# RetNet attention into a gated MLP on one core: two product groups moved ahead of the sixth piece's transposition

## The chip, the cores and the metric

The kernel runs on one core of one Trainium2 chip, in one launch. The metric is device microseconds of one execution; less is better. Each time quoted as a median comes from several executions of the same program.

## The reference

Batch 8, 8 heads, 576 positions, head dimension 64. Each head has a decay of its own, and there is no softmax. The attention's result is laid out as 4608 tokens by 512 features and goes through an MLP with 2048 hidden features. The weights arrive in double precision.

```
gamma = 1 - 2 ** (-5 - arange(H))
scores = q @ k.T / sqrt(D)
Dmat = where(i >= j, gamma ** (i - j), 0)
x = ((scores * Dmat) @ v)          # B,H,S,D -> (B*S, H*D)
h = x @ w_in
g = h * erf(softplus(h))
out = g @ w_out
```

## The kernel before

**Pieces.** The 4608 tokens are cut into 36 pieces of 128 tokens. Two batches make nine pieces: four of 128 positions for each batch, and one that holds the last 64 positions of both. Below, T5 is the transposition of the piece with index 5, which is the sixth piece; S5 are its scores and O5 its outputs.

**Stages of the attention.** Three functions handle a piece. `transposes(i)` turns q and k with four TensorE transposes each (line 332), which ScalarE copies out of PSUM (lines 334 and 338). It also has GpSimd weigh the piece's v (line 313), and at its end it issues the load of q for piece i+2. `scores(i)` multiplies the turned k and q on TensorE (line 347), and VectorE masks them into `sT`. `outputs(i)` multiplies `sT` with v (line 365), adds the product of q and the state carried from earlier pieces (line 376), and computes the new state's sum (line 388). VectorE then scales the results into the tile `x`, and the load of k and v for piece i+3 is issued. The list `stages` holds these calls in the order T0, S0, T1, O0, S1, T2, O1, S2 and so on; `attend` runs the next one. For piece 5 and piece 7 two neighbours are swapped, so that the list runs T5, O4, S5, O5, T6, S6.

**Blocks of the MLP.** Four pieces fill one tile `x` of 512 tokens, called a chunk here. There are nine chunks and four groups of 256 + 256 hidden features, so 36 blocks. Most blocks compute x @ w_in by seven products of half size (line 496). The first block of all, `firsts[0]`, uses `plain()` (line 550) instead: four accumulators in PSUM, `p0`, `p1`, `pe` and `pg`, each for one half of the tokens and one half of the group's features. The sum over 512 input features is cut into four quarters, `dc` = 0 to 3. In each quarter four groups of matmuls follow one another, one for each accumulator, and `plain()` yields after each group. A group is four matmuls of 128x256; the trace has two records for each matmul. Groups `p0` and `p1` read the tokens of pieces 0 and 1, groups `pe` and `pg` the tokens of pieces 2 and 3.

**Weights.** `load_weights` issues the transfer of one part of the weights into the tile `wraw`. `rounding()` turns a part from double to single precision in steps: ScalarE (lines 254 and 255), then VectorE (lines 259, 263, 267, 272), then a product and a sum (lines 274 and 275), on VectorE for the first group's w_in and on GpSimd otherwise. Each quarter of the first block needs one part, in `wa`.

**Order of the work.** Engines run their instructions in program order, and the program order around the change is written by hand, as one letter per call:

```
for what in "alkakakawkakakawwaa3awa2aaa5ppappa5wwppa5ppawappwcppa5ppaaapp5s":
    if what == "a":
        attend(done[0] + 1)
    elif what == "p":
        next(products)
```

Here `a` is the next stage of the attention, `p` the next group of the first block, `w` the issue of a weight part, a digit so many steps of rounding, `k` two small matmuls that only keep TensorE working, `l` a load of k and v, `c` a load of constants, and `s` the store of the first chunk. All loads named here are issued on SyncE, in program order.

Of the kernel before, what the change touches and what calls it, by code (L numbers as in the profile page):

```python
# [54 lines left out]
def kernel(  # L55
# [94 lines left out]
    def load(i, names="qkv"):  # L150
        if i < len(pieces):
            t = loaded.setdefault(i, {})
            for name in names:
                src = {"q": q, "k": k, "v": v}[name]
                if name == "q" and i < SQUARES:
                    t["q"] = load_rows(i, "q", q, 2)
                elif name == "q":
                    t["qs"] = load_squares(i, "q", q)
                    if i >= SQUARES_K:
                        t["ks"] = load_squares(i, "k", k)  # L160
                elif name == "v" or i < SQUARES_K or len(pieces[i]) == 1:
                    t[name] = load_rows(i, name, src, 4)
# [69 lines left out]
    def load_weights():  # L232
        part = next(coming, None)
        if part is not None:
            t = wraw.tile([P, 2 * WP], UINT32, tag="wraw", name="wraw")
            for rows, src in part[0]:
                nc.sync.dma_start(out=t[rows].rearrange("p (h f) -> p h f", h=2), in_=src)
            words.append((t, *part[1:]))
# [49 lines left out]
    def round_weights(n=1):  # L288
        for _ in range(n):
            next(round_step, None)  # L290
# [159 lines left out]
    def attend(upto):  # L450
        while done[0] < min(upto, len(stages)):
            of, i = stages[done[0]]
            of(i)
            done[0] += 1
# [9 lines left out]
    def store_x(c):  # L464
        nc.sync.dma_start(out=xd[c], in_=x[0, c][:, :n_dc])
# [269 lines left out]
    def keep_busy(n):  # L735
        for _ in range(n):
            nc.tensor.matmul(idle[:, :P], lhsT=ones, rhs=ones, start=True, stop=True)
# [13 lines left out]

    for what in "alkakakawkakakawwaa3awa2aaa5ppappa5wwppa5ppawappwcppa5ppaaapp5s":
        if what == "a":
            attend(done[0] + 1)
        elif what == "p":
            next(products)
        elif what == "s":
            store_x(0)  # L760
        elif what == "l":
            load(2, "kv")
        elif what == "c":
            nc.sync.dma_start(out=cst[:, CONST_FIRST:], in_=consts[:, CONST_FIRST:])
        elif what == "w":
            load_weights()
        elif what == "k":
            keep_busy(2)
        else:
            round_weights(int(what))  # L770
# [93 lines left out]
```

## Time and profile before

| what | value |
|---|---|
| median of 6 runs | 1029.72 us |
| the six runs, in order of size | 1028.46, 1029.05, 1029.40, 1030.04, 1030.07, 1030.37 us |
| profiled execution, its time | 1030.37 us |
| profiled execution, its span | 1028.6 us |
| TensorE busy | 1019.3 us, 99% of the span |
| VectorE busy | 669.0 us, 65% |
| ScalarE busy | 390.3 us, 38% |
| GpSimd busy | 122.5 us, 12% |
| mean granted TensorE clock | 0.998 |

The span is the time from the first to the last recorded instruction of the profiled execution; its own time is 1.77 us longer, for what lies around the span. All positions given below count from the span's start. PE stands for TensorE, PEld for its weight loads, DVE for VectorE, ACT for ScalarE, POOL for GpSimd, SP for SyncE. A busy PE is not PE at full rate: matmuls are pipelined, and the ends in the trace are modelled. A line of the timeline gives start, duration, engine, line of the code, operation, what is written from what, shapes and the count of records; the bracket at its end gives idle time of the engine before it and what ended it.

### The profile page before, as it was taken

The numbers are of one execution on the slowest core, as the hardware profiler recorded it, in microseconds if no ns is written. First come the engines' busy times: TensorE is split into PE (matmuls) and PEld (weight loads), VectorE is DVE, ScalarE is ACT, GpSimd is POOL, SyncE is SP. The second block draws the span as 40 slices with busy tenths as digits, with TensorE's granted clock in tenths as the row PEclk, the third lists the DMA queues.
The fourth block names the chain that finished last, engine by engine and source line by source line (L and its number), as shares of the span: only waits on it lengthen the run. The fifth ranks groups of instructions, "written<-read, shape, count | busy, mean of one in ns | idle before, by whom it ended". The sixth has DMA issues, their size and how long they took to land.

```text
span 1028.6 us, 15959 instructions
## 1 busy us (share of the span) xinstructions
PE 1019.3 (99%) x6348; PEld 876.4 (85%) x6348; DVE 669.0 (65%) x1062; ACT 390.3 (38%) x481; POOL 122.5 (12%) x122
## 2 busy tenths in 40 slices
PE   9999999999999999999999999999999999999998
PEld 7788888888888888888888888888888888888887
DVE  3759877877876666666566666666667655555555
ACT  2354133232244544343443344444443333333332
POOL 2133121222311110000001001100100000000000
PEclk9999999999999999999999999999999999999999
DMA  9996979989984444444445344444433334444434
GB/s 198 205 241 143 245 172 230 232 173 249 239 178 153 159 144 143 144 166 161 163 143 174 136 143 147 159 166 144 143 123 123 123 125 131 131 132 131 128 85 120
DMA packets 146986, 165.76 MB, mean 161 GB/s; under 512 B 97376, under 2 KB 121568, under 8 KB 138848
## 3 DMA queue, kind: packets, MB, share of 16 engines
q1 hardware_dynamic: 144832, 163.57, 56.2%
q10 hardware_dynamic: 2080, 1.18, 0.5%
q8 instruction: 50, 0.82, 0.4%
q14 instruction: 24, 0.20, 0.1%
HBM read 117.52 MB, written 47.19 MB: 160 GB/s over the span
## 4 chain that ended last, share of the span: by engine, by line
PE 90%; DMA 4%; DVE 3%; SPq 2%; issue 1%; POOL 1%; ACT 0%; DVEq 0%; POOLq 0%
PE a L604 23%; PE a L496 22%; PE g L604 12%; PE g L496 11%; PE e L496 6%; PE e L604 6%; PE s L347 3%; PE o L365 3%; PE o L388 1%; PE o L376 1%; DMA raw_v<-in_v_dram 1%; DMA raw_ks<-in_k_dram 1%; SPq L147 1%; PE f L668 1%; DMA raw_k<-in_k_dram 1%
## 5 line engine op out<-in xcount | busy, mean ns | idle before, releaser
L496 PE MATMUL a<-x,wa 128*128 128x256 f32 x1088 | 258.3, 380 | 0.0
L496 PEld LDWEIGHTS a<-x,wa 128*128 128x128 f32 x1088 | 205.8, 190 | 28.5
L604 PE MATMUL a<-wb,s 128*128 128x256 f32 x840 | 200.0, 381 | 0.0
L604 PEld LDWEIGHTS a<-wb,s 128*128 128x128 f32 x840 | 158.4, 190 | 22.9 <-ACT o L618 0.7
L99 DVE TENSOR_TENSOR t<-g,t 128x512 f32<-128x512 f32 x68 | 46.9, 690 | 150.7 <-ACT t L526 113.1
L496 PE MATMUL g<-x,wa 128*128 128x256 f32 x544 | 129.2, 380 | 0.0
L496 PEld LDWEIGHTS g<-x,wa 128*128 128x128 f32 x544 | 102.8, 190 | 14.4
L99 DVE TENSOR_TENSOR o<-a,o 128x512 f32<-128x512 f32 x104 | 71.4, 686 | 46.5 <-PE a L604 46.5
L521 ACT COPY t<-a 128x512 f32<-128x512 f32 x34 | 19.9, 586 | 188.2 <-PE a L496 188.2
L99 DVE TENSOR_TENSOR t<-t,s 128x1024 f32<-128x1024 f32 x72 | 88.8, 1273 | 0.0
L565 ACT ACTIVATE s<-t 128x1024 f32<-128x1024 f32 x72 | 72.1, 1048 | 28.4 <-DVE t L99 28.4
L274 POOL TENSOR_TENSOR wraw<-wraw 128x512 f32<-128x512 f32 x28 | 29.4, 1051 | 439.5 <-DVE wraw L272 177.9
L99 DVE TENSOR_TENSOR x<-x 128x512 f32<-128x512 f32 x115 | 75.8, 692 | 1.2
L532 ACT COPY t<-a 128x512 f32<-128x512 f32 x34 | 19.9, 586 | 144.3 <-PE a L496 144.3
L569 ACT ACTIVATE s<-s 128x1024 f32<-128x1024 f32 x72 | 72.2, 1049 | 0.4
L604 PE MATMUL g<-wb,s 128*128 128x256 f32 x280 | 66.7, 381 | 0.2 <-DVE t L99 0.2
L604 PE MATMUL e<-wb,t 128*128 128x256 f32 x280 | 66.6, 381 | 0.0
L604 PE MATMUL a<-wb,t 128*128 128x256 f32 x280 | 66.6, 381 | 0.0
L604 PE MATMUL g<-wb,t 128*128 128x256 f32 x280 | 66.4, 380 | 0.0
L496 PE MATMUL e<-x,wa 128*128 128x256 f32 x272 | 64.8, 381 | 0.0
L99 DVE TENSOR_TENSOR sT<-s,cst 128x512 f32<-128x512 f32 x72 | 46.1, 681 | 27.8 <-PE s L347 27.8
L99 DVE TENSOR_TENSOR o<-g,o 128x512 f32<-128x512 f32 x70 | 47.9, 684 | 21.5 <-ACT o L618 18.8
(86 smaller groups left out, 1249.5 us busy)
## 6 DMA issues: line engine op xcount, KB each, us to landing
od<-o SPq DMA_DIRECT2D x54, 512.0 KB, 3.3
x<-xd SPq DMA_DIRECT2D x27, 1024.0 KB, 4.8
o<-od SPq DMA_DIRECT2D x27, 1024.0 KB, 5.0
raw_qs<-in_q_dram SPq DMA_DIRECT2D x96, 112.0 KB, 4.4
raw_ks<-in_k_dram SPq DMA_DIRECT2D x84, 112.0 KB, 4.2
xd<-x SPq DMA_DIRECT2D x9, 1024.0 KB, 5.3
raw_v<-in_v_dram SPq DMA_DIRECT2D x64, 128.0 KB, 4.5
wraw<-in_moe_w_in_dram SPq DMA_DIRECT2D x32, 256.0 KB, 5.8
```

The costliest lines, as they stand in the source:

```text
L99: nc.vector.tensor_tensor(out=out, in0=in0, in1=in1, op=op)
L147: queue.dma_start(out=t[r0 : r0 + n, e::2, :], in_=heads.rearrange("h p d -> p h d"))
L274: engine.tensor_tensor(out=r_f, in0=high_f, in1=r_f, op=ALU.mult)
L347: nc.tensor.matmul(ps[e][:, p, :], lhsT=t["kT"][heads[e], p, :], rhs=t["qT"][heads[e], p, :], start=True, stop=True)
L365: nc.tensor.matmul(o[p % 2][heads[(e + p) % 2], p // 2, :], lhsT=t["v"][:, 2 * p + e, :], rhs=t["sT"][:, e, p, :], start=(p < 2), stop=(no ...
L376: nc.tensor.matmul(o[p % 2][heads[(e + p) % 2], p // 2, r0 : r0 + m], lhsT=state[heads[e], p, :], rhs=t["qT"][heads[e], p, r0 : r0 + m], s ...
L496: nc.tensor.matmul(acc[:, j * TH : (j + 1) * TH], lhsT=weights["wa", self.g][:, a, d, j * P : (j + 1) * P], rhs=x[self.g, self.c][a][:, d, :],
L521: nc.scalar.copy(out=self.t1[:, 1], in_=self.a)
L532: nc.scalar.copy(out=self.t2[:, 0], in_=self.a)
L565: nc.scalar.activation(self.s[:, j], t, AF.Softplus)
L569: nc.scalar.activation(self.s[:, j], self.s[:, j], AF.Erf)
L604: nc.tensor.matmul(acc[:, tp, :], lhsT=left[:, j * TH + tp * P : j * TH + (tp + 1) * P], rhs=weights["wb", self.g][:, b, j, :], start=(sta ...
```

## The change

One string changes. After the fourth piece's outputs and the scores of the fifth piece, the kernel before calls two groups of the first block's first quarter (`p0`, `p1`), then T5, then the other two groups (`pe`, `pg`), then O4. The kernel after calls all four groups first, then T5, then O4.

```
-    for what in "alkakakawkakakawwaa3awa2aaa5ppappa5wwppa5ppawappwcppa5ppaaapp5s":
+    for what in "alkakakawkakakawwaa3awa2aaa5ppppaa5wwppa5ppawappwcppa5ppaaapp5s":
         if what == "a":
             attend(done[0] + 1)
         elif what == "p":
```

On TensorE eight matmuls (two groups) and eight transposes exchange places. Nothing is added or removed. The instructions of VectorE, ScalarE, GpSimd and SyncE keep their order.

More of the change, by code (lines that the diff above doesn't have):

```diff
@@ L750 @@
     products = firsts[0].plain()
-    for what in "alkakakawkakakawwaa3awa2aaa5ppappa5wwppa5ppawappwcppa5ppaaapp5s":
+    for what in "alkakakawkakakawwaa3awa2aaa5ppppaa5wwppa5ppawappwcppa5ppaaapp5s":
         if what == "a":
```

## The prediction

> **What bounds the kernel now.** I read the page first. TensorE is busy for 1019.3 of 1028.6 us, and the chain that ended last lies on it for nine tenths:
>
> ```profile
> PE 1019.3 (99%) x6348; PEld 876.4 (85%) x6348; DVE 669.0 (65%) x1062; ACT 390.3 (38%) x481; POOL 122.5 (12%) x122
> PE 90%; DMA 4%; DVE 3%; SPq 2%; issue 1%; POOL 1%; ACT 0%; DVEq 0%; POOLq 0%
> ```
>
> So an edit pays only where TensorE stands still or runs slowly, and what it saves there is kept only if nothing later holds TensorE back. The waits of TensorE over the whole span are few. The longest is 1.6 us, for the load of q at line 332, and that is T5. The next view is TensorE's timeline around it:
>
> ```profile
> 28.62 1.16 PE L347 MATMUL s<-qT,kT 64*128 64x128 f32 x16
> 29.71 1.99 PE L550 MATMUL p<-x,wa 128*128 128x256 f32 x8
> 33.27 0.63 PE L332 MATMUL pt_q<-ident,raw_q 128*128 128x128 f32 x4 [1.57 <-DMA raw_q<-in_q_dram]
> 34.45 0.75 PE L332 MATMUL pt_k<-ident,raw_k 128*128 128x128 f32 x4 [0.56 <-DMA raw_k<-in_k_dram]
> 35.00 1.92 PE L550 MATMUL pe<-x,wa 128*128 128x256 f32 x4
> 36.71 1.78 PE L550 MATMUL pg<-x,wa 128*128 128x256 f32 x4
> 38.42 1.09 PE L365 MATMUL o<-sT,raw_v 128*64 128x128 f32 x16
> ...
> 48.70 1.89 PE L550 MATMUL p<-x,wa 128*128 128x256 f32 x8
> 50.43 1.03 PE L550 MATMUL pe<-x,wa 128*128 128x256 f32 x4
> 51.30 1.03 PE L550 MATMUL pg<-x,wa 128*128 128x256 f32 x4
> 52.25 1.16 PE L347 MATMUL s<-qT,kT 64*128 64x128 f32 x16
> ```
>
> Two things are to be seen. TensorE idles 1.57 + 0.56 = 2.13 us for the sixth piece's q and k. And `pe` and `pg` behind T5 take 38.42 - 35.00 = 3.42 us, where the same two groups of a later quarter, at 50.43, take 52.25 - 50.43 = 1.82 us, and a full set of four groups 52.25 - 48.70 = 3.55 us. The third view explains this: stretches of 3.41 us laid where the granted clock changes (columns: length, PE busy, granted clock, DMA share, GB/s).
>
> ```profile
> 7.52:10.93 3.41, 2.71 (x26) 1.00 1.34 218
> 28.00:31.41 3.41, 3.41 (x44) 1.00 1.23 212
> 31.41:34.82 3.41, 1.29 (x10) 1.00 0.80 161
> 34.82:38.24 3.42, 3.42 (x11) 0.50 0.90 182
> 38.24:41.65 3.41, 3.41 (x41) 1.00 1.11 209
> ```
>
> TensorE was busy for only 1.29 us of 31.41 to 34.82, and then the clock was halved from 34.82 to 38.24: just where `pe` and `pg` ran. A stretch that was busy for 2.71 us, at 7.52, was followed by full clock.
>
> **The change, part by part.** *The two groups go into the wait.* `p0` starts at 29.71 as now. Four groups at full clock take 3.55 us, so T5's first transpose is due at 29.71 + 3.55 = 33.26. Its q let the present one start at 33.27. The first wait is filled to the last hundredth, and T5 is not delayed at all. The wait for k stays: the k transposes start at 34.45, as now. *O4 follows directly.* From the first k transpose to the next instruction it takes 0.43 us at 48.27 and 0.53 us at 55.61; I take 0.50. O4 then starts at 34.95 instead of 38.42, which is 3.47 us earlier. At full clock the two groups would have taken about 3.55 - 1.82 = 1.73 to 1.82 us behind T5; so some 1.75 us of the gain is the filled wait and 1.7 us the half clock that does not come.
>
> *Does the clock stay up?* In 31.41 to 34.82 TensorE would now be busy from 31.41 to 33.26 (1.85 us), for the q transposes (0.63) and for the part of the k transposes before 34.82 (0.37): 2.85 us, above the 2.71 that kept full clock. I therefore count no slow stretch. A bound: if it came all the same, O4 and what follows would lose half of 3.41, 1.7 us.
>
> [...]
>
> *The wait that moves.* `pe` and `pg` read the third and fourth piece's tokens, so `pe` now waits itself for VectorE's scaling of O3. That ended at 30.23 + 0.41 = 30.64, and `pe` is due at 29.71 + 1.73 = 31.44: 0.8 us in hand. Were this cover gone, each microsecond would cost one until the k transposes' 34.45 absorb it.
>
> *Queues that T5 is moved past.* T5 also issues GpSimd's weighing of v (no place changed: it waited until 36.32 for its load) and SyncE's load of q for piece 7, which needs T5's q transposes done. SyncE gets to that load only at 39.17, 5.3 us after those transposes; they end at the same 33.9 in both kernels. So no later load is put off. ScalarE's copy of k stays at about 35.3, tied to the load.
>
> *What is late next.* O4's inputs are ready: its `sT` was written by 31.83 and its v weighed by 29.1. Behind it comes this run on VectorE and ScalarE:
>
> ```profile
> 35.30 0.58 ACT L338 COPY kT<-pt_k 128x512 f32<-128x512 f32 x1 [0.72 <-PE pt_k L332]
> 35.78 0.66 ACT L254 ACTIVATE wa<-wraw 128x512 f32<-128x512 f32 x1
> 39.57 0.42 DVE L99 TENSOR_TENSOR x<-o,cst 128x256 f32<-128x256 f32 x1 [4.23 <-PE o L365]
> 40.70 0.41 DVE L259 TENSOR_SCALAR wa<-wa 128x512 f32<-128x512 f32 x1
> 44.21 1.28 DVE L99 TENSOR_TENSOR sT<-s,cst 128x512 f32<-128x512 f32 x2
> ```
>
> VectorE stood idle for 4.23 us before 39.57, waiting for O4, so it can start 3.47 us earlier. It then rounds the third weight part, from 40.70 - 3.47 = 37.2; ScalarE has that ready by 35.78 + 0.66 = 36.44, with 0.8 us in hand. The second part, needed by `p0` of the next quarter at 39.91 - 3.47 = 36.44, is finished at 34.65 + 0.69 = 35.34. `sT` of piece 5 and O5, which waits about half a microsecond for it now, move together. Then come the loads for T6, now at 47.78 and then at 44.3: SyncE issued its k by 35.96, and transfers there take 5.7 us, so they are in by 41.7. The fourth weight part reached ScalarE at 39.21, and VectorE wants it at 45.41 - 3.47 = 41.9. The first part of w_out is issued by 43.7 and takes 5.4, in by 49; ScalarE's use moves from 49.48 to 49.0 at best, but VectorE wants it only at 54.65 - 3.47 = 51.2. From 60 to 91 VectorE is tight (the chain runs over it), but it starts those stretches behind TensorE and ScalarE, which move too. From 91 on TensorE has almost no wait left. I count nothing given back; the bound is all of it, which is the third case below.
>
> **The sum.** 1030.37 - 3.47 = 1026.90 us for an execution like the profiled one, its span 1025.1. That execution is 0.65 us above the median of 1029.72, and the six runs spread over 1.91 us. If the half clock struck in only some of them, the others gain about 1.75: the upper three (mean 1030.16) would come to 1026.7, the lower three (mean 1028.97) to 1027.2. Both meet at 1026.9, which I forecast; its own range is 1026.0 to 1027.8.
>
> **The rivals.** *Only the wait pays.* The half clock is rare without the profiler, or comes back after T5, or a part of it is absorbed. Then 1.75 us off the median gives 1028.0, off the profiled run 1028.6. For it: one execution shows the clock. Against it: the spread of 1.9 us is about what such a stretch costs.
>
> *The load was never the end of it.* VectorE's backlog from 73 to 93, or a load tied to the clock on the wall, takes the place of the wait, and the time stays near 1029.7. For it: the chain of waits passes over VectorE's rounding there. Against it: the margins above, and 3.45 us idle on VectorE at 53.45.
>
> *The rounding holds its place (slower).* If the third part's rounding stayed at 40.70 to 44.29 in spite of O4's earlier end, `sT` of piece 5 would stay at about 45.5, and TensorE, there at 41.5, would stand 3.4 us longer than now. That gives back 3.4, and a stretch with so little work would halve the clock for another 3.41 us, for 1.7 more: 1030.37 - 3.47 + 3.4 + 1.7 = 1032.0. It loses against the profiled run from an added wait of 3.47 - 1.7 = 1.8 us on. Against it: VectorE's 4.23 us idle and ScalarE's early rows.
>
> **How the numbers follow.** About 0.2%, 2.06 us, is what a measurement of this kernel can tell from no change; that is 1027.66 on the fast side. The full gain has 0.68, only the wait 0.18, nothing kept 0.10, slower 0.04. Faster by over 0.2% takes the first and a tenth of the second: 0.70. Within it: 0.26. Slower: 0.04. The range takes in the first two cases and part of the third, with half a microsecond of spread below: 1025.6 to 1029.2.
>
> **What would show it.** In the changed kernel's timeline the four groups run from 29.7 to 33.3, the wait for q is gone or under 0.2 us, the one for k stays near 0.5, and O4 starts near 35.0. The granted clock stays at 1.00 through 38. O5 waits about half a microsecond for `sT` as now, and the second product block and all later ones come 3.5 us earlier. The forecast is wrong if a wait at O5, T6 or the masks between 73 and 93 grows by over a microsecond, or if 0.50 stands anywhere in the granted clock before the end.

## The result and the profile after

The kernel after takes 1027.37 us in the median of 17 runs (1026.1 to 1031.25), the kernel before, over all runs up to then, 1030.0 us in the median of 38 (1027.89 to 1032.61). The ratio is 0.9976, with a 95% interval of 0.9969 to 0.9984; that is 2.5 us less, from 1.6 to 3.2. The forecast was 1026.9 us, with a range of 1025.6 to 1029.2.

The profiled execution of the kernel after took 1027.61 us, its span 1025.8 us. These are the lines of TensorE's timeline that answer to those shown of before (a group is two matmuls with two records each, so x4 is one group, and it is four matmuls that change places with the eight transposes):

```profile
29.72 1.99 PE L550 MATMUL p<-x,wa 128*128 128x256 f32 x8
31.55 1.03 PE L550 MATMUL pe<-x,wa 128*128 128x256 f32 x4
32.41 1.03 PE L550 MATMUL pg<-x,wa 128*128 128x256 f32 x4
34.37 0.63 PE L332 MATMUL pt_q<-ident,raw_q 128*128 128x128 f32 x4 [0.93 <-DMA raw_q<-in_q_dram]
35.40 0.63 PE L332 MATMUL pt_k<-ident,raw_k 128*128 128x128 f32 x4 [0.40 <-DMA raw_k<-in_k_dram]
35.95 1.09 PE L365 MATMUL o<-sT,raw_v 128*64 128x128 f32 x16
...
42.79 0.40 PE L365 MATMUL o<-sT,raw_v 128*64 128x128 f32 x2 [0.34 <-issue]
...
50.05 1.16 PE L347 MATMUL s<-qT,kT 64*128 64x128 f32 x16
```

`pe` and `pg` now run at full rate (1.03 us each by their records, against 1.92 and 1.78 before) in the time in which TensorE stood still. The wait for q has shrunk from 1.57 to 0.93 us and is not gone, because in this execution q landed about a microsecond later than in the profiled one of before (34.37 against 33.27). O4 starts 2.47 us earlier (35.95 against 38.42), the scores at line 347 near 50 are 2.20 us earlier (50.05 against 52.25), and the span is 2.8 us shorter. Most of the rest of that last figure comes in small steps much later: in the profile of before TensorE waits for VectorE by 0.28 us at the scores at 236.54 and by 0.20 us at the products at 255.40; after, both waits are gone, and one of 0.23 us stands at the scores at 272.62.

The third view, stretches of 3.41 us (length, PE busy, granted clock, DMA share, GB/s), laid in phase with the one change of the granted clock at the start of this trace:

```profile
31.67:35.08 3.41, 2.40 (x13) 1.00 0.83 155
35.08:38.50 3.42, 3.10 (x41) 1.00 0.85 179
```

The least busy of them has 2.40 us of work, and the clock stays at 1.00 up to the drain at the end of the kernel (0.50 from 1024.95). The prediction had 2.85 us for its stretch. Most of the difference is the later load: the k transposes start at 35.40, behind the end of the stretch, where 0.37 us of them were counted in.

### The profile page after: what moved, and what is told of

It reads as the page before. It is cut to its first block, busy times and chain, and to the rows that moved or that the text cites. A ratio compares the mean times of both kernels' runs of the same rounds, so it can differ in the third digit from the quotient of the medians.

```text
span 1025.8 us, 15958 instructions
## 1 busy us (share of the span) xinstructions
PE 1017.3 (99%) x6348; PEld 875.5 (85%) x6348; DVE 668.7 (65%) x1062; ACT 390.2 (38%) x481; POOL 122.6 (12%) x122
## 4 chain that ended last, share of the span: by engine, by line
PE 88%; DMA 6%; DVE 2%; SPq 2%; ACT 1%; issue 1%; POOL 1%; DVEq 0%; POOLq 0%; ACTq 0%
PE a L604 23%; PE a L496 22%; PE g L496 11%; PE g L604 11%; PE e L604 6%; PE e L496 5%; PE s L347 2%; PE o L365 2%; DMA raw_v<-in_v_dram 2%; DMA raw_qs<-in_q_dram 1%; PE o L388 1%; PE o L376 1%; SPq L147 1%; DMA raw_ks<-in_k_dram 1%; PE f L668 1%
```

## The experiments

There were two explanations to tell apart. Theory A: the gain has two parts, the wait that is filled and the stretch at half clock that no longer follows it. Rival B: only the filled wait pays, and the half clock in one profiled execution was an accident. Every timed execution comes with its mean granted TensorE clock; one stretch of 3.41 us at half clock lowers it to 0.998, which makes the two countable. (A mean of 0.999 need not have such a stretch: in experiments 6 and 7 it is a half clock in the last 1.1 and 1.5 us, behind the last matmul.)

**1. The kernel before, unchanged**

> The kernel before, unchanged, for the granted clock of each of its executions. Theory A (an idle wait of about 2.1 us ahead of the sixth piece's transposition, and behind it a half clock of 3.41 us that costs 1.7 us more, in a good part of the executions): at least a third of the executions show a mean granted clock of 0.998 (one half-clock stretch, 3.41 x 0.5 / 1028 = 0.0017), and these are 1 to 2 us longer than those at 0.999 to 1.0. Rival B (only the wait paid, the half clock in the profiled execution was an accident): hardly any execution is at 0.998, or those that are take no longer. Time against the kernel before: 0 +- 0.7 us.

Time: ratio 0.9994 (0.9985 to 1.0003). Together with the runs of before beside it there are 34 executions: 20 at 0.998 or lower, with a mean of 1030.57 us, and 14 above, with a mean of 1028.92. Over all three sets of runs in this study there are 71 executions of the kernel before: 38 at 0.998 or lower (mean 1030.59) and 33 above (1028.92). So the half clock strikes in 54% of the executions, and these are 1.67 us longer in the mean. Its profile caught it again, with the stretches in another phase:

```profile
32.17:35.59 3.42, 1.57 (x11) 1.00 0.65 145
35.59:39.00 3.41, 3.41 (x15) 0.50 0.87 163
```

TensorE was busy for 1.57 us of the first stretch and ran at half clock in the second. Rival B falls on this: the half clock is common and has its price.

**2. Idle work in the wait**

```
-    "...aaa5ppappa5ww..."
+    "...aaa5ppfappa5ww..."
+        elif what == "f":
+            spare = ps_at.tile([P, NP, P], FP32, tag="at", name="spare")
+            for _ in range(6):
+                nc.tensor.matmul(spare[:, 0, :], lhsT=ones, rhs=ones, start=True, stop=True)
```

> The kernel before, with six small 128x128 matmuls on constants put into the wait, ahead of the sixth piece's transposition; the order is otherwise that of before. They take about 1.3 us where TensorE stood still for 1.57 us, so they do no useful work and delay nothing. Theory A: the stretch from 31.4 to 34.8 is now busy for about 2.6 us, the clock stays at 1.00, and the kernel is 0.8 to 1.7 us faster than before (all of it from the clock). Rival B: no gain, 0 +- 0.4 us.

Ratio 0.9986 (0.9976 to 0.9995), 1.4 us less than before; none of 11 executions at 0.998. The timeline of its profile:

```profile
31.29 1.50 PE L772 MATMUL spare<-ones 128*128 128x128 f32 x12
33.22 0.63 PE L332 MATMUL pt_q<-ident,raw_q 128*128 128x128 f32 x4 [0.43 <-DMA raw_q<-in_q_dram]
34.70 1.03 PE L550 MATMUL pe<-x,wa 128*128 128x256 f32 x4
```

T5 starts when its load is in, as before; the matmuls ahead of it produce nothing that is used. Yet `pe` takes 1.03 us for its four records and not 1.92, and the kernel is faster. This is the clock's part alone. The mean of the 11 executions, 1028.68 us, is that of the kernel before without the half clock (1028.92) within the spread of the runs.

**3. Three groups ahead of T5**

```
-    "...aaa5ppappa5ww..."
+    "...aaa5pppapa5ww..."
```

> Three of the four groups ahead of the sixth piece's transposition, the fourth behind it. Theory A: each group moved into the wait saves its 0.87 us as long as the load is not yet in, and one group is enough to keep the clock up (the stretch is then busy for about 2.0 us): 1.7 to 2.6 us faster than before, the part left over being the fourth group's 0.87 us. Rival B: 0.87 us faster. If 2.0 us of work are too few to keep the clock, also about 0.9.

Ratio 0.9972 (0.996 to 0.9984), median 1027.57 us, none of 6 executions at 0.998. One group was enough to keep the clock, with 2.31 us of work in the stretch over the wait. T5 still waited 0.69 us for q and 0.41 us for k, and O4 started at 35.75. It came out no slower than the kernel after, although the fourth group fits into that wait. The profiles show how this can be: O4 starts at 35.00 in experiment 5, 0.75 us earlier than here, and yet the span is 1025.8 us there and 1025.5 us here. "What was late next", below, has the place where it was lost.

**4. O4 ahead of T5 as well**

```
-        if i in (PC + 1, 2 * PC - 1):
+        if i in (PC, PC + 1, 2 * PC - 1):        # with the string of after
```

> The kernel after, with the outputs of the fifth piece (O4, 1.5 us on TensorE) also ahead of the sixth piece's transposition. In the profile of after, that transposition still waited 0.93 us for q and 0.40 us for k. If these waits are the rest of the loss, O4 fills them and the kernel is 0.9 to 1.5 us faster than the kernel after, 3.4 to 4.1 us faster than before. If VectorE's work behind O4 decides (scaling, rounding of the third weight part, mask of piece 5), O5 waits longer for its mask and less than 0.5 us is gained over after. If the later load of piece 7's q, which now comes behind its k and v, is missed at T7, a wait at T7 appears.

Ratio 0.9967 (0.9955 to 0.998), median 1026.8 us. T5 no longer waits, but O5 does:

```profile
36.79 0.45 DVE L259 TENSOR_SCALAR wa<-wa 128x512 f32<-128x512 f32 x1 [0.95 <-ACT wa L254]
...
41.12 1.64 PE L365 MATMUL o<-sT,raw_v 128*64 128x128 f32 x16 [0.92 <-issue]
```

The mask of piece 5 stands behind the rounding of the third weight part on VectorE, and that waits for ScalarE, whose step stands behind T5's copies: VectorE idled for 0.95 us ahead of line 259. This is the mechanism of the second expectation. The gain over the kernel after is 0.6 us by the medians and 0.9 us by the two ratios, so its size does not decide between the two expectations. The third one's wait at T7 did not occur. One of 6 executions was at 0.998.

**5. The kernel after, unchanged**

> The kernel after, unchanged, for the granted clock of its executions and as the neighbour of the three that follow. Theory A (the filled wait, 1.6 us, and the half clock that does not come, 1.65 us in those executions that have it): at most one execution in eight at a mean clock of 0.998; those of the kernel before, beside it, at 0.998 in about half, and 1.65 us longer there than the others. Time: 2.2 to 2.9 us faster than before. Rival B (only the wait): as many half-clock executions as before, 1.6 us faster.

Ratio 0.9976 (0.9967 to 0.9986), median 1027.44 us, none of 9 executions at 0.998; beside it the kernel before had 8 of 19 there, with a mean of 1030.66 against 1029.17 us for the other 11. With the result's own executions (18 are listed with their clock) the kernel after has 1 of 27 at 0.998. This profile has T5 as the prediction had it:

```profile
33.43 0.63 PE L332 MATMUL pt_q<-ident,raw_q 128*128 128x128 f32 x4 [0.17 <-DMA raw_q<-in_q_dram]
34.44 0.63 PE L332 MATMUL pt_k<-ident,raw_k 128*128 128x128 f32 x4 [0.38 <-DMA raw_k<-in_k_dram]
35.00 1.09 PE L365 MATMUL o<-sT,raw_v 128*64 128x128 f32 x16
```

**6. ScalarE's step earlier**

```
-    "...aaa5ppppaa5ww..."
+    "...aaa5ppppa1a4ww..."        # with the swap of experiment 4
```

> The fourth experiment's order (four groups and O4 ahead of the sixth piece's transposition) with ScalarE's first step on the third weight part taken ahead of that piece's copies. There VectorE stood idle for 0.95 us before line 259, waiting for ScalarE, and O5 waited 0.92 us for the mask behind it. If ScalarE's place in this queue is what now ends last, VectorE starts line 259 at once, O5's wait falls to 0.2 us or less, and the kernel is 0.7 to 0.9 us faster than that one, 4.0 to 4.5 us faster than before. If the wait at O5 is VectorE's own length of work, it stays over 0.6 us and nothing is gained.

Ratio 0.9962 (0.995 to 0.9975), median 1025.64 us, 1.8 us below the kernel after on the same chip (1.4 us by the ratios). VectorE did start line 259 at once, at 36.04. But O5 still waited 0.72 us, where 0.2 or less was expected. These are the two lines of VectorE and GpSimd that show why:

```profile
36.95 1.41 DVE L267 SCALAR_TENSOR_TENSOR wa<-wraw,wa 128x512 uint32<-128x512 uint32 x1
36.50 1.32 POOL L313 TENSOR_TENSOR raw_v<-raw_v,cst 128x512 f32<-128x512 f32 x1 [6.51 <-DMA raw_v<-in_v_dram]
```

The step of line 267 takes 0.69 us elsewhere; here it began while GpSimd weighed v and took 1.41. The wait at O5 is of just that size, so it is the wait of the second expectation that stayed. Whether this kernel is faster than that of experiment 4 is not settled by the two intervals.

**7. O4 in the wait in place of the product groups**

```
-    "...aaa5ppppaa5ww..."
+    "...aaa5ppaapp5ww..."        # with the swap of experiment 4
```

> The two product groups stay behind the sixth piece's transposition as in the kernel before; the fifth piece's outputs (O4, 1.5 us) go into the wait in their place. Theory A: what fills the wait does not matter, only that it is work whose inputs are there. O4 takes 1.5 of the 1.57 us, the clock stays at 1.00, and the kernel is 2.1 to 2.8 us faster than before, as far as after. Against it, if the product groups had to go first for the sake of what follows on VectorE or ScalarE: under 1.2 us faster.

Ratio 0.9966 (0.9953 to 0.9979), median 1026.04 us, none of 5 executions at 0.998. As far as 5 executions can tell, what fills the wait does not matter. The profile shows a late load (T5 waited 1.32 us for q in spite of O4), and so it has the least busy stretch around T5 that kept the clock. The end of the same execution has one that did not; there are no transposes in it:

```profile
31.70:35.11 3.41, 1.76 (x33) 1.00 0.64 126
35.11:38.52 3.41, 3.34 (x18) 1.00 0.85 177
...
1021.57:1024.98 3.41, 1.32 (x7) 1.00 0.81 226
1024.98:1026.45 1.47, 0.00 (x0) 0.50 0.04 12
```

**8. The load earlier, the order on TensorE as before**

```
-    "...kakakawwaa3awa2aaa5ppappa5ww..."
+    "...kakakawaa3awwa2aaa5ppappa5ww..."
```

> The order of the kernel before on TensorE; on SyncE one weight part (512 KB) is loaded behind the sixth piece's q, k and v instead of ahead of them. SyncE issues that q some 1.5 us earlier, so it lands about 1.5 us earlier, and T5 waits 0 to 0.5 us instead of 1.57. Theory A: 1.2 to 1.7 us from the wait and about 1 us from the clock, 2.0 to 2.8 us faster than before with no instruction of TensorE moved. If the transfers are bound by bandwidth in a way that the order does not change, or if the third weight part now comes too late for VectorE, the wait shows up again at T5 or O5 and less than 1 us is gained.

The profiled execution is 3.07 us below that of before (1027.30 us), but the median of 11 runs is 1028.79 and the ratio 0.9994 (0.9983 to 1.0004): no gain that can be told. In the profile T5 starts at 31.27 without a wait for q, and the third weight part is late instead, so the wait has gone to O5:

```profile
42.50 1.64 PE L365 MATMUL o<-sT,raw_v 128*64 128x128 f32 x16 [1.37 <-issue]
```

3 of the 11 executions are at 0.998, with a mean of 1030.83; the other 8 have 1028.21. So the wait that was moved, not removed, seems to bring the half clock along.

**9. The kernel of experiment 6 again**

> The sixth experiment's kernel (four groups and O4 ahead of the sixth piece's transposition, ScalarE's step on the third weight part earlier) again, as neighbour of the next. 3.2 to 4.2 us faster than before, at most one execution in eight at a clock of 0.998.

Ratio 0.9968 (0.9958 to 0.9979), median 1026.15 us, none of 8 executions at 0.998. The ratios of both sets, 0.9962 and 0.9968, lie below the kernel after's 0.9976 by 0.8 to 1.4 us.

**10. The mask ahead of the rounding**

```
-    "...aaa5ppppa1a4wwppa5ppawapp..."
+    "...aaa5ppppa1awwppa4ppa5wapp..."        # with the swap of experiment 4
```

> That kernel with piece 5's mask ahead of the rounding of the third weight part on VectorE, and the rounding of the fourth part behind piece 5's outputs. O5 waited there for the mask, by 0.72 us and half a microsecond more inside its first matmuls, because the rounding stood in front and one step of it took 1.41 us instead of 0.69 beside GpSimd's weighing of v. Theory: with the mask first, O5 does not wait at all and the kernel is 0.7 to 1.3 us faster than its neighbour, 4.2 to 5.3 us faster than before. Rival: VectorE's work has now to be caught up behind O5, the rounded third and fourth weight parts come later, and the first block's third or fourth quarter waits for them by as much: no gain, and a wait at line 550 near 44 or 49.

Ratio 0.9965 (0.9953 to 0.9978), median 1025.70 us. The same as experiment 9 as far as can be told; the rival named in the expectation came true:

```profile
40.73 1.09 PE L365 MATMUL o<-sT,raw_v 128*64 128x128 f32 x16
...
49.37 1.99 PE L550 MATMUL p<-x,wa 128*128 128x256 f32 x8 [0.76 <-DVE wa L275]
```

O5 waits no more, and the fourth quarter of the first block waits 0.76 us for its rounded weights.

**11. Idle work ahead of O5, on experiment 8's order**

```
-    "...aaa5ppappa5wwppa5ppawapp..."
+    "...aaa5ppappa5wwppa5ppfawapp..."        # f as in experiment 2, five matmuls
```

> The eighth experiment's kernel (one weight part loaded behind the sixth piece) with five small matmuls on constants ahead of O5, where it waited 1.37 us for the mask. In its timed executions 3 of 11 were at a mean clock of 0.998 and 2.5 us longer than the others. Theory A: the new wait at O5 brings the half clock back in some executions; filled with 1.1 us of idle work, no execution is at 0.998 and the time is 1.6 to 2.4 us faster than before, against 0.7 there. Rival: the clock of those executions had another cause; then the share at 0.998 stays near a quarter and nothing is gained.

Ratio 0.9987 (0.9978 to 0.9997), median 1028.68 us, none of 11 executions at 0.998. The direction is that of theory A, the size is below the expected 1.6 us, since in its profile O5 still waits 1.01 us behind the idle work. Three of 11 against none of 11 is too few to prove the cause by itself.

## Why the prediction was right

**The wait and its filling.** The sum had 1.75 us for it. Taken among executions without the half clock, the kernel before has a mean of 1028.92 us (33 of them) and the kernel after 1027.37 us (26): 1.55 us. Two steps were mis-sized; how much of the 0.2 us each of them took is not shown. One is "the first wait is filled to the last hundredth". It rested on one landing time. T5's q let it start at 33.27 in the profile of before, 33.43 in experiment 5 and 34.37 in the profile of after, and where it comes late a wait remains: 0.93 us there. O4 at 34.95, as predicted, is what experiment 5 has with 35.00; the profile of after has 35.95. The other is "I count nothing given back", below.

**The half clock.** The sum had 1.7 us for it; 38 of 71 executions of before have it, and it costs 1.67 us. In the kernel after 1 of 27 has it. Averaged, that is 0.54 x 1.67 = 0.9 us less 0.06 us, and with the filled wait 1.55 + 0.84 = 2.4 us, against a measured 2.5. The prediction knew the half clock from one execution. It worked through the case that only some are struck with the upper three of six run times (mean 1030.16) and the lower three (1028.97); the two classes have 1030.59 and 1028.92, so that guess was good, without a clock to rest on. Experiment 2 shows this part alone, with no order changed.

**The clock stays up.** The prediction asked only that a stretch be as busy as one seen to keep full clock, 2.71 us. The runs narrow this: after 1.29 and 1.57 us of work in 3.41, and 1.32 us at the end of experiment 7, the clock was halved; after 1.76 (experiment 7), 2.31 (experiment 3) and 2.40 us (after) it was not. Whether transposes count as work, as both figures of the prediction, 2.85 and 2.71 us, took them to, experiment 7 answers in one execution: the stretch that kept the clock has 0.63 us of q transposes in its 1.76 us, so 1.13 us of other work, less than the 1.32 us without transposes that did not keep it. Here they counted. In the two profiles of before the half clock runs from 34.82 and from 35.59, each time for 3.41 us: 0.77 us later in the second, where T5 starts only 0.22 us later (33.49 against 33.27). So it did not keep a fixed place in the program. That a stretch can lie anywhere over the waits, and that this is why the same program has the half clock in some executions only, is the author's estimate: both profiled ones were struck, so none shows the other case. By that estimate, worked out from the matmul rows of the two, of all the places where a stretch of 3.41 us can lie over the waits, between 36% (the first profile, a limit of 1.57 us of work) and 74% (the second, 1.76 us) would bring the half clock, and 54% was measured. Gaps of 1.57 and 1.88 us, each with a shorter one behind it (0.56 and 0.53 us), were enough here.

**The wait that moved, the queues.** `pe` waited for nothing, and no wait appeared at T6 or T7, as predicted. SyncE issued T5's load of q for piece 7 at 39.53 in experiment 5 and at 40.20 in the profile of after, against 39.17 before. The weight part that it issues earlier is later by about as much (32.97 and 33.47 against 32.49), so it is the queue that ran later, and not T5's place that put the load off.

**What was late next.** "I count nothing given back" did not hold. In the profile of after 2.47 us are won at O4 and 2.21 us at O5. These lines, of VectorE and GpSimd in the kernel after, show where 0.26 us went:

```profile
37.59 1.04 POOL L313 TENSOR_TENSOR raw_v<-raw_v,cst 128x512 f32<-128x512 f32 x1 [7.19 <-PE o L388]
37.10 0.42 DVE L99 TENSOR_TENSOR x<-o,cst 128x256 f32<-128x256 f32 x1 [1.52 <-PE o L365]
38.23 0.68 DVE L259 TENSOR_SCALAR wa<-wa 128x512 f32<-128x512 f32 x1
42.00 1.28 DVE L99 TENSOR_TENSOR sT<-s,cst 128x512 f32<-128x512 f32 x2
```

Line 259 took 0.41 us in the profile of before and 0.68 us here: VectorE works earlier now and meets GpSimd's weighing of v, which started later here (37.59 against 36.32 before). In experiment 5 the weighing started at 35.98, the two did not meet, line 259 took 0.41 us, and O5 came 3.42 us earlier, as O4 did.

But experiment 5 gave back more, and much later, where the prediction saw "almost no wait left" on TensorE. The first two lines are of experiment 5, the last two of before:

```profile
260.35 1.13 DVE L326 STREAM_TRANSPOSE kT<-raw_ks 128x512 f32<-128x512 f32 x1 [0.72 <-DMA raw_ks<-in_k_dram]
272.52 1.16 PE L347 MATMUL s<-qT,kT 64*128 64x128 f32 x16 [0.68 <-DVE kT L326]
...
263.06 1.13 DVE L326 STREAM_TRANSPOSE kT<-raw_ks 128x512 f32<-128x512 f32 x1
275.24 1.16 PE L347 MATMUL s<-qT,kT 64*128 64x128 f32 x16
```

Up to there everything ran some 3.4 us earlier. VectorE, which turns the later pieces itself (line 326), then came to a load of k that had not landed, for which it had not waited in before. From 260.35 to 272.38 it was busy for 11.99 of 12.03 us, so it could not catch up, and TensorE's scores waited for it. What is left from there on is 275.24 - 272.52 = 2.72 us, and the span is 1025.8 us and not the predicted 1025.1. So the rival of a load that does not move along came true for 0.7 of 3.42 us in this execution; the profile of after has its 0.23 us at the same scores.

The slower rival, in which the rounding keeps its place, did not occur in the kernel after; experiments 4, 8 and 10 show its milder form, once the wait at T5 is gone.

**What stays open.** Why the sixth piece's q lands up to a microsecond later in some executions of nearly the same transfers was not tried, and neither was an earlier load of the k for which VectorE waits at 260. The one execution of the kernel after at a clock of 0.998 has no profile.

## What to carry to other kernels

Price an idle gap of TensorE twice: by its own length, and by a half clock that may follow it. Here gaps of at most 1.57 and 1.88 us were followed by 3.41 us at half clock, and the executions that had it were 1.67 us longer in the mean. When a single profile shows a stretch at half clock, look at the clock of many executions before it enters the sum in full, since here it struck in 54% of them. A gap that is filled shows the next wait in the chain, and here three further waits of 0.7 to 1.4 us stood close behind (O5's mask, ScalarE's step, the rounded weights), so that each further step bought less. Look for the next wait over the whole kernel, too: in experiment 5 it stood 240 us behind the change. The order of experiment 6 was the best repeated one, with medians of 1025.64 and 1026.15 us.

## What the runs showed of the hardware

Some steps of VectorE that start while GpSimd's multiplication at line 313 runs end later: line 267 took 1.41 us and not 0.69 (experiment 6), line 259 took 0.68 (after) and 1.15 us (experiment 7) and not 0.42, and line 275 took 1.42 and not 0.69 (experiment 8). In experiment 6 GpSimd ran until 36.50 + 1.32 = 37.82 and line 267 ended at 38.36, 0.54 us later, not far from its whole length of 0.69. The scaling of TensorE's results at line 99 was not slowed: in experiment 5 it started at 36.15 beside a multiplication of 35.98 to 37.02 and took its usual 0.42 us, and in the profile of after it took 0.41 us from 37.90 beside one of 37.59 to 38.63. Why some steps are slowed and others not, no run shows.

A few matmuls on constants, placed in a wait, paid 1.4 us without moving any useful work (experiment 2). There a stretch of 3.41 us with 2.65 us of work, the matmuls on constants among it, was followed by a clock of 1.00, and `pe` took 1.03 us; in the profile of before one with 1.29 us was followed by 0.50, and `pe` took 1.92 us.
